# Dividing a kernel's softmax exponentials between ScalarE and VectorE, by a schedule fixed when the program is built

## The chip, the cores and the metric

One core of a Trainium2 chip runs the whole program. The time is device microseconds of one execution. A time quoted below is the median of a kernel's runs; all runs of both kernels, and of every experiment timed in rounds, were in the fast state. Two experiments were run once only, so that their state is unknown. TensorE is called PE, its weight loads PEld, VectorE DVE, ScalarE ACT, GpSimd POOL, and SyncE, which issues most transfers, SP.

## The reference

Four layers on x of 2048 x 512: spectral, attention, spectral, attention, each with a layernorm ahead and a residual add behind. The spectral layers do not change. The attention has 32 query heads of 16 columns and a single key and value head:

```python
def _B_ref(x, wq, wk, wv, wo):
    B, S, D = x.shape            # 1, 2048, 512
    H = 32
    Dh = D // H                  # 16
    q = (x @ wq) ...             # to (B, H, S, Dh)
    k = x @ wk
    v = x @ wv
    scores = jnp.einsum("bhqd,bkd->bhqk", q, k) * (Dh ** -0.5)
    p = _softmax(scores, axis=-1)
    o = jnp.einsum("bhqk,bkd->bhqd", p, v)
    return o ... @ wo
...
x = x + _A_ref(_layernorm(x, axis=-1), A_w_r, A_w_i)
x = x + _B_ref(_layernorm(x, axis=-1), B_wq, B_wk, B_wv, B_wo)
# and both once more
```

A layer has 32 x 2048 x 2048 exponentials: 2048 units of 128 keys x 512 queries. No maximum is subtracted before the exponential.

## The kernel before

Scores are laid out with keys on the partitions. Three units share one PSUM tile and one exponential; its output is the stationary operand of the value matmuls, whose 17th column sums the denominators. `Kv` holds the 16 key columns in one of eight places with zeros in the other rows, so that a full 128-row matmul gives one head. The tile library orders the instructions.

```python
psc = ctx2.enter_context(tc.tile_pool(name="psc", bufs=2, space=bass.MemoryType.PSUM))
...
for gi0 in range(0, len(units), G):                    # G = 3
    grp = units[gi0:gi0 + G]
    sc = psc.tile([P, G, 512], F32, tag="sc")
    for uj, (pidx, kc, hh, qb) in enumerate(grp):
        ...
        nc.tensor.matmul(sc[:, uj, :], lhsT=Kv[:, v, kc * P:(kc + 1) * P],
                         rhs=QT[:, g, qb * 512:(qb + 1) * 512],
                         start=True, stop=True, skip_group_check=True)
    e = expp.tile([P, G * 512], BF, tag="e")
    nc.scalar.activation(out=e[:, 0:ng * 512], in_=sc[:, 0:ng, :]...,
                         func=ACT.Exp, scale=SCALE)
    for uj, unit in enumerate(grp):
        emit_pv(unit, e[:, uj * 512:(uj + 1) * 512], gi0 + uj)   # 4 matmuls, 17 columns each
```

The output projection comes after all of this, as do the residual adds and the layernorm of the next layer, which takes its square root on ACT:

```python
def layernorm_tile(nc, lnpool, tabs, x_ap, xn_ap, on_act=True, use_pool=False):
    ...  # statistics on DVE, into mv
    nc.scalar.activation(out=rstd, in_=mv[:, 1:2], func=ACT.Sqrt, bias=tabs["eps"], scale=1.0)
    nc.vector.reciprocal(rstd, rstd)
    ...  # nb = -mean * rstd, on DVE
    # then xn = x * rstd + nb: on POOL, ACT or DVE
```

The softmax here doesn't subtract the row's maximum and nothing guards it: scores larger than these inputs give would overflow.

## Time and profile before

| | before |
|---|---|
| median of 4 runs | 2298.5 us (2297.8 to 2299.0) |
| span of the profiled run, granted clock | 2296.3 us, 0.979 |
| start to the first exponential | 193 us |
| exponentials, first and second attention layer | 940 and 942 us |
| from the first layer's last exponential to the second's first | 197 us |
| last exponential to the end | 24.6 us |

The windows view gives, for a stretch of the span, the length, each engine's busy time with its number of instructions in brackets, then the granted PE clock, the DMA share and GB/s. These are the two stretches of exponentials, the second cut a microsecond wide:

```profile
core 0: us, PE busy (x) PEld busy (x) DVE busy (x) ACT busy (x) POOL busy (x), PEclk, DMA share, GB/s
193.00:1133.00 940.00, 776.93 (x10282) 357.87 (x10280) 35.69 (x72) 931.90 (x684) 19.42 (x30) 1.00 0.03 4
1330.00:2273.00 943.00, 776.34 (x10286) 357.87 (x10283) 36.53 (x75) 932.33 (x683) 19.43 (x30) 1.00 0.03 4
```

ACT is 99% busy and DVE 4%. This is the whole case for the change: one engine full, another, which can also do arithmetic on every element, idle beside it.

### The profile page before, as it was taken

What the parts mean: (1) busy time and instruction counts of PE and PEld (TensorE: products, weight loads), DVE (VectorE), ACT (ScalarE), POOL (GpSimd) and SP (SyncE); (2) the same over time, 40 slices, a digit from 0 to 9 for tenths busy, and PEclk for the clock granted to TensorE, in tenths of its full rate; (3) what the DMA queues carried; (4) which work ended last, traced back from release to release, by engine and by line L of the source; (5) the groups of instructions that cost most, each with busy time, mean ns of one, the idle gap of its engine ahead of it and who ended that gap; (6) DMA issues with size and microseconds to landing.
All of it is one profiled execution on the core that took longest, in us unless ns stands there. A gap on an engine that the chain in (4) does not pass through costs nothing.

```text
span 2296.3 us, 49219 instructions
## 1 busy us (share of the span) xinstructions
PE 1883.0 (82%) x22176; PEld 864.0 (38%) x22176; DVE 354.5 (15%) x1019; ACT 2059.4 (90%) x1768; POOL 92.1 (4%) x143
## 2 busy tenths in 40 slices
PE   6798888888888888888787988888888888888887
PEld 3234333333333333333342433343333333333333
DVE  6861000000000000000168500000000000000002
ACT  6448999999999999999864489999999999999995
POOL 2011000000000000000000200000000000000000
PEclk9799999999999999999997999999999999999999
DMA  4000000000000000000000000000000000000001
GB/s 133 0 1 20 4 4 4 4 4 4 4 4 4 4 4 4 4 4 4 4 1 0 10 10 4 4 4 4 4 4 4 4 4 4 4 4 4 4 4 40
DMA packets 46818, 19.12 MB, mean 8 GB/s; under 512 B 37376, under 2 KB 43664, under 8 KB 46608
## 3 DMA queue, kind: packets, MB, share of 16 engines
q1 hardware_dynamic: 42464, 11.11, 2.3%
q0 software_dynamic: 4144, 4.87, 1.4%
q8 instruction: 173, 2.83, 0.5%
q14 instruction: 37, 0.30, 0.0%
HBM read 8.63 MB, written 2.10 MB: 5 GB/s over the span
## 4 chain that ended last, share of the span: by engine, by line
ACT 77%; PE 13%; DVE 6%; issue 4%; DMA 1%; ACTq 0%; POOL 0%; DVEq 0%
ACT e L431 76%; PE ps L253 2%; PE ps L145 1%; PE ps L160 1%; PE ps L158 1%; PE sc L427 1%; PE ps L228 1%; PE pv_new L309 1%; DVE stats L84 1%; PE ps L443 1%; DVE m L204 1%; DVE m L210 1%; DVE m L205 0%; DVE Zpk L206 0%; DVE Zsw L212 0%
## 5 line engine op out<-in xcount | busy, mean ns | idle before, releaser
L431 ACT ACTIVATE e<-sc 128x1536 bf16<-128x1536 f32 (+1 forms) x1366 | 1864.2, 1449 | 24.0 <-PE sc L427 11.0
L427 PE MATMUL sc<-QT,Kv 128*128 128x512 bf16 x4096 | 1107.8, 377 | 11.1 <-ACT e L431 10.1
L410 PE MATMUL pv_new<-vaug,e 128*128 128x17 bf16 x16384 | 625.5, 172 | 318.4 <-ACT e L431 316.1
L410 PEld LDWEIGHTS <-e 128*128 128x128 bf16 x16384 | 502.3, 96 | 968.9 <-ACT e L431 954.9
L427 PEld LDWEIGHTS <-Kv 128*128 128x128 bf16 x4096 | 299.1, 96 | 184.3 <-issue 15.2
L387 DVE RECIPROCAL rden<-pv_new 128x32 f32<-128x32 f32 x32 | 11.5, 358 | 1787.9 <-PE pv_new L410 1787.9
L399 POOL DMA_DIRECT2D OQ<-oTp x64 | 41.4, 651 | 1855.4 <-DVE oTp L396 1853.4
L88 ACT ACTIVATE rstd<-mv,eps 128x1 f32<-128x1 f32 x64 | 17.5, 287 | 57.6 <-DVE mv L86 55.6
L116 PE MATMUL ps<-tab_ident,xn_sb 128*128 128x128 bf16 x256 | 26.7, 275 | 32.1 <-ACT xn_sb L97 18.5
L198 ACT CAST Xs<-ps 128x512 bf16<-128x512 f32 x32 | 18.8, 588 | 37.8 <-DVE m L211 37.5
L158 PE MATMUL ps<-Ppk,tab_C 128*128 128x512 bf16 x128 | 48.5, 379 | 0.0
L160 PE MATMUL ps<-Psw,tab_S 128*128 128x512 bf16 x128 | 48.5, 379 | 0.0
L253 PE MATMUL ps<-tab_C,Dpk 128*128 128x512 bf16 x128 | 48.5, 379 | 0.0
L443 PE MATMUL ps<-WO,OQ 128*128 128x512 bf16 x128 | 36.7, 426 | 11.7 <-DVE x_sb L445 5.3
L196 PE MATMUL ps<-Bpk,tab_ident 128*128 128x512 bf16 x64 | 26.5, 493 | 22.5 <-ACT Xs L200 22.5
L84 DVE BATCH_NORM_STATS2 stats<-x_sb 128x6 f32<-128x512 bf16 x64 | 42.1, 675 | 6.4 <-DMA x_sb<-in_A_x_dram 6.3
L97 ACT ACTIVATE xn_sb<-x_sb,nb,rstd 128x512 bf16<-128x512 bf16 x48 | 37.2, 806 | 5.3 <-DVE nb L91 5.3
L172 ACT ACTIVATE tmp<-ps,tab_TWS 128x512 bf16<-128x512 f32 x24 | 16.5, 687 | 23.9 <-PE ps L160 17.1
L253 PEld LDWEIGHTS <-Dpk 128*128 128x128 bf16 x256 | 25.1, 98 | 30.2 <-DVE Dpk L238 0.4
L116 PEld LDWEIGHTS <-xn_sb 128*128 128x128 bf16 x256 | 21.9, 124 | 37.9 <-ACT xn_sb L97 23.7
L228 PE MATMUL ps<-Zpk,tab_ident 128*128 128x512 bf16 x64 | 26.0, 477 | 11.7 <-DVE Dpk L238 4.4
L255 ACT CAST AT<-ps 128x512 bf16<-128x512 f32 x32 | 18.5, 579 | 18.2 <-PE ps L253 18.2
(89 smaller groups left out, 838.7 us busy)
## 6 DMA issues: line engine op xcount, KB each, us to landing
x_sb<-in_A_x_dram SPq DMA_DIRECT2D x1, 2048.0 KB, 10.7
OQ<-oTp SPq DMA_DIRECT2D x64, 32.0 KB, 2.4
OQ<-oTp POOLq DMA_DIRECT2D x64, 32.0 KB, 2.7
wr_sb<-in_A_w_r_dram SPq DMA_DIRECT2D x1, 1024.0 KB, 6.5
win_sb<-in_A_w_i_dram SPq DMA_DIRECT2D x1, 1024.0 KB, 10.0
out_dram<-x_sb SPq DMA_DIRECT2D x8, 128.0 KB, 1.7
out_dram<-x_sb POOLq DMA_DIRECT2D x8, 128.0 KB, 2.1
wq_sb<-in_B_wq_dram POOLq DMA_DIRECT2D x1, 512.0 KB, 9.0
```

The source lines that it names most:

```text
L84: nc.vector.bn_stats(stats, x_ap)
L97: nc.scalar.activation(out=xn_ap, in_=x_ap, func=ACT.Identity, bias=nb, scale=rstd)
L116: nc.tensor.transpose(ps[:, tt, cc, :], xn_sb[:, r_, t_, cc * P:(cc + 1) * P], ident)
L158: nc.tensor.matmul(ps, lhsT=C512[:, r, m * P:(m + 1) * P], rhs=Ppk[:, rt, :], start=(k == 0), stop=False)
L160: nc.tensor.matmul(ps, lhsT=S512[:, r, m * P:(m + 1) * P], rhs=Psw[:, rt, :], start=False, stop=(r == R - 1))
L228: nc.tensor.matmul(ps, lhsT=lt, rhs=src[:, a, :], start=(k2 == 0), stop=(k2 == T - 1))
L253: nc.tensor.matmul(ps, lhsT=lt, rhs=tab[:, m, :], start=(k == 0), stop=(k == 7))
L399: eng.dma_start(out=OQ[32 * kq:32 * kq + 32, q4, :, 32 * pb:32 * pb + 32], in_=oTp[32 * pb:32 * pb + 32, :, :])
L410: nc.tensor.matmul(pv[:, hh, k * 17:k * 17 + 17], lhsT=eu[:, qq * P:(qq + 1) * P], rhs=vaug[:, kc, :], start=first, stop=last, skip_group_ ...
L427: nc.tensor.matmul(sc[:, uj, :], lhsT=Kv[:, v, kc * P:(kc + 1) * P], rhs=QT[:, g, qb * 512:(qb + 1) * 512], start=True, stop=True, skip_gr ...
L431: nc.scalar.activation(out=e[:, 0:ng * 512], in_=sc[:, 0:ng, :].rearrange("p a b -> p (a b)"), func=ACT.Exp, scale=SCALE)
L443: nc.tensor.matmul(ps, lhsT=OQ[:, q4, k, :], rhs=WO4[:, q4, :], start=(q4 == 0), stop=(q4 == nq - 1))
```

## The change

The intent is to give part of the exponentials to DVE. DVE is given no exponential; it computes a line into int16 whose bits, read as bf16, are approximately a power of two. A second copy, shifted by 64 (half an octave) and weighted in the value matmul, halves the bend of that line's error. Four heads of one key block make a "quad"; a small time model in Python hands each of a layer's 512 quads to ACT or DVE, and pins the order of PE, ACT and DVE instructions to what it worked out. Score matmuls shrink to 64 rows (two can run side by side), value matmuls to 32 output rows (four side by side). Denominators are spread by transfers; projection, residual add and layernorm move into the loop. The core of the diff:

```diff
+NTERM = 2
+SH = (0, 64)
+SW = (1.0, 0.70703125)
+EXP_LN = 0.7317
+Y_MUL = float(SCALE * np.log2(np.e) * 128.0)
+Y_ADD = 127.0 * 128.0
...
+class Plan:
+    NA, ND = 2, 4
+    MM, CHANGE, LAT = 0.217, 0.1, 0.2
+    T_EXP, T_READ, T_16, T_DEN, T_ON = 0.94, 0.61, 0.62, 0.5, 0.7
+    D_RECIP, D_ON = 3.0, 5.0
...
+    def scores(u, out):
+        pin(nc.tensor.matmul(out, lhsT=KT[64 * (i // 2):64 * (i // 2) + 64, 2 * (i % 2) + half, kc * P:(kc + 1) * P],
+                             rhs=QT[64 * (i // 2):64 * (i // 2) + 64, g, qb * 512:(qb + 1) * 512], ...))
+    def pv(u, j, e):
+        pin(nc.tensor.matmul(acc[32 * i:32 * i + 32, :], lhsT=V3[:, kc, j, :], rhs=e, ...))
...
+    def finish(qb, s):
+        pin(nc.scalar.copy(out=den, in_=acc))
+        for i in range(4):
+            nc.sync.dma_start(out=dq[32 * i:32 * i + 32, :], in_=den[32 * i + DH:32 * i + DH + 1, :]...)
+        later.append((st["act"] + M.D_RECIP, lambda: recip(qb, s, den, dq, rb)))
...
+    def score_pair():                       # ACT
+        pin(nc.scalar.activation(out=e, in_=sa, func=ACT.Exp, bias=EXP_LN, scale=SCALE))
+        st["act"] = max(st["act"], done) + M.T_EXP
+    def score_single():                     # DVE
+        pin(nc.vector.tensor_scalar(out=t0[:, n, :], in0=sd, scalar1=Y_MUL, scalar2=Y_ADD, op0=ALU.mult, op1=ALU.add))
+        st["dve"] = max(st["dve"], done) + M.T_READ
+        if n == ND - 1:
+            pin(nc.vector.tensor_scalar(out=t2, in0=t0, scalar1=float(SH[1]), scalar2=None, op0=ALU.add))
+            st["dve"] += M.T_16
...
-            for gi0 in range(0, len(units), G):      # and all that is shown of the kernel before
...
-    wka = const.tile([P, NC, P], BF, name="wka")
+    wka = const.tile([P, NC, 4, P], BF, name="wka")   # key projection four times, once per placement
```

`pin` keeps an instruction at its place in the program's order. The numbers in `Plan` are what the time model believes; they change no instruction, only the order and the split.

## The prediction

> **What bounds the kernel now.** I read the page's shares first, then the chain of waits that ends last, then the groups, then the timeline of two microseconds in mid-attention. The page's head and its chain:
>
> ```profile
> PE 1883.0 (82%) x22176; PEld 864.0 (38%) x22176; DVE 354.5 (15%) x1019; ACT 2059.4 (90%) x1768; POOL 92.1 (4%) x143
> ...
> ACT  6448999999999999999864489999999999999995
> ...
> ACT 77%; PE 13%; DVE 6%; issue 4%; DMA 1%; ACTq 0%; POOL 0%; DVEq 0%
> ```
>
> ACT is full in two long plateaus, the two attention layers, and is 77% of the chain. DVE is idle there (a 0 in nearly every slice). The groups, with shapes kept apart, say which instruction it is and what PE does meanwhile:
>
> ```profile
> L431 ACT ACTIVATE e<-sc 128x1536 bf16<-128x1536 f32 x1364 | 1862.3, 1450 | 24.0 <-PE sc L427 11.0 <-PE pv_new L410 9.7 <-ACT e L431 1.9
> L427 PE MATMUL sc<-QT,Kv 128*128 128x512 bf16 x4096 | 1107.8, 377 | 11.1 <-ACT e L431 10.1 <-DVE vaug L341 1.0
> L410 PE MATMUL pv_new<-vaug,e 128*128 128x17 bf16 x16384 | 625.5, 172 | 318.4 <-ACT e L431 316.1
> ...
> L431 ACT ACTIVATE e<-sc 128x1024 bf16<-128x1024 f32 x2 | 2.0, 1017 | 0.0
> ```
>
> The exponentials of 4096 units of 128x512 (2048 a layer) are the bound: in all that time ACT idled 24.0 us, while the value matmuls waited 316 us for it. The timeline of the steady state gives the period:
>
> ```profile
> 599.47 5.54 ACT L431 ACTIVATE e<-sc 128x1536 bf16<-128x1536 f32 x4
> ...
> 601.26 0.34 PEld L427 LDWEIGHTS <-Kv 128*128 128x128 bf16 x3
> 601.29 0.81 PE L427 MATMUL sc<-QT,Kv 128*128 128x512 bf16 x3
> 602.33 0.37 PEld L410 LDWEIGHTS <-e 128*128 128x128 bf16 x12 [0.73 <-ACT e L431]
> 602.34 0.46 PE L410 MATMUL pv_new<-vaug,e 128*128 128x17 bf16 x12 [0.24 <-ACT e L431]
> ```
>
> Score bursts start at 601.29 and 602.65, so three units cost 1.36 us, 0.455 each; an exponential of 1450 ns overlaps its neighbour by about 0.09. The first exponential of layer one starts at 192.99 and the last ends at 1132.83; in layer two they run from 1329.91 to about 2271.7. That is 940 + 942 = 1882 us of attention core, and 2298 - 1882 = 416 us of everything else.
>
> **What the skill says.** Four places bear on it.
> - "VectorE: DVE Perf Modes", section "The perf-mode tier table": a one-source operation on 16-bit data in SBUF runs at four elements a cycle, while fp32 from PSUM gets one. The trace agrees: a 128x4096 bf16 tensor_scalar takes 1227 ns, a 128x512 cast out of PSUM 692 ns.
> - "TensorEngine Tiling (Array Packing)", "Key Properties": tiles run independently, but changing the tiling mode drains the engine. Nothing before shows it, as all its matmuls are 128*128.
> - "TensorE: Matmul & The Clock Gate", "Measured speedup vs the span model": four row tiles gave 3.07 times and three column tiles 2.38 times, not 4 and 3. Not seen here either.
> - "ScalarE: Activation LUTs", "What ACT_TABLE_LOAD costs": 1283 ns for a load plus 1380 ns of drain. The trace has 1283 ns for the load, but no drain beside it: the last exponential ends at 1132.83, the load runs from 1132.85 for 1.28 us; another, from 180.00, is followed by an exponential at 181.30. I use 1.3 us.
>
> **The change part by part.**
>
> (a) Exponentials. Four heads of one key block and query block form a quad; there are 512 quads a layer. A greedy schedule, fixed when the program is built, gives each to ACT or to DVE. On ACT a quad is two activations of 128x1024: 1.017 - 0.09 = 0.93 us each (its source constant says 0.94), so 1.88 us. On DVE it is four linear maps out of PSUM into int16 (the bits are read back as bf16, a piecewise-linear power of two) and one 128x2048 add of 64 that makes a second, half-octave-shifted copy. Rows: 692 ns for 512 columns from PSUM; two back-to-back residual adds took 1.29 us, so consecutive ones cost about 0.61. The 2048-column add by the 4096-column row: (1227 - 160)/2 + 160 - 80 of overlap = about 0.61. A DVE quad is 4 x 0.61 + 0.61 = 3.05 us. ACT alone did a quad in 1.82. Together: 1/1.88 + 1/3.05 = 0.86 quads a microsecond, 595 us a layer if neither ever waits.
>
> (b) Added work on those two engines, a layer: on ACT 32 copies of the accumulator (0.5 each) and 12 query copies (0.5), 22 us; on DVE 32 normalisations (0.69), 32 small reciprocals (0.2) and 12 of the 16 residual adds inside the loop (0.68), 37 us, plus in the first attention layer the layernorm's statistics (675 + 166 + 152 + 198 ns, 12 times, 14 us). DVE's old reciprocal, multiply and transpose work (58 us in all) goes, but was hidden.
>
> (c) TensorE. Scores become 64-row matmuls, two of which can run at once; value matmuls become 32-column ones with 512 moving columns, four at once, a term for ACT units and two for DVE units. 512 columns at full clock take 0.217 (3.69 us for 16 in the old key projection is 0.23 with its edges). ACT quad: 2 x 0.217 + 0.217 = 0.65. DVE quad: its scores are issued one per free slot, often unpaired, 4 x 0.217, + 2 x 0.217 = 1.30. At the ratio of (a), 0.62 DVE quads to an ACT quad, that is 1.46 us per 1.88 us. With perhaps three mode changes in that time at 0.1 us (the source's constant) and rows of four at 3.07 rather than 4 times, TensorE asks for 1.46 + 0.3 + 0.15 = 1.9 us. This is an estimate, and it says that TensorE has no slack left: it becomes a third, equally loaded engine that the two others must queue for.
>
> (d) What that does to the slots. DVE has two one-bank score slots. A freed slot needs 0.217 for the matmul and about 0.2 until DVE sees it, against 0.61 until the other slot is used up: 0.19 us of slack, less than a value burst with two mode changes (0.4 or more). ACT has 0.93 - 0.42 = 0.5. So I take DVE at 83% busy and ACT at 93%, both within the time T of a layer. Less the added work (ACT 22, about 3%; DVE 37, about 5%, and 3% waiting on reciprocal transfers, see e): ACT 0.90/1.88 = 0.479, DVE 0.75/3.05 = 0.246; 0.725 quads a microsecond: 706 us a layer.
>
> (e) Transfers. The denominators go through four one-row transfers, a reciprocal, a store to DRAM and a broadcast read. SP takes 1.26 us to issue two transfers, and one lands after 2.4 us: the fourth lands at 3 x 0.63 + 2.4 = 4.3 us, where the schedule puts the reciprocal at 3.0. The store and read, 2 x 2.4, about fill their allowed 5.0. About 1 us of DVE waiting in 32 stages is the 3% above.
>
> (f) Table loads. Projection and layernorm now run inside the loop. In the first attention layer each of 12 square roots falls among exponentials: 2 x 1.3 + 0.29, and 0.8 for the normalising activation: 12 x 3.7 = 44 us on ACT, with the other two engines soon starved behind it. The second layer only writes out.
>
> (g) Edges. Key projection grows from 16 to 64 matmuls: +48 x 0.216 = +10 us a layer; the query projection up front stays at 16; the key rearrangement by transfers (3.1 us) goes. At the end 1132.8 to 1160.5, 28 us, becomes the last denominator chain (0.6 + 4.3 + 0.2 + 5 + 0.7) and four projections of 8 matmuls (8 us), 19 to 20 us: -8. Edges come to about 0.
>
> Sum: 416 + 706 + (706 + 44) = 1872; I say 1870 us, 19% less.
>
> **Rivals.**
> - Packed matmuls do not overlap, and TensorE becomes the bound: per layer 2048 x 0.217 + 2048 x 1.36 x 0.217 = 444 + 604 = 1050 us, plus changes, so about 1150: 416 + 2300 = 2700 us. For: nothing before shows overlap. Against: the skill's measured packing. I give it 3%.
> - The schedule works nearly as planned, both elementwise engines 95% full: 595/0.95 + 25 = 650 a layer, 44 less hidden: 1740 us. For: the source's constants agree with my rows. Against: (c) leaves TensorE no room, and order is fixed on all engines, so one late operand holds everyone.
> - Waits replace the bound: each schedule slip (reciprocal at 3.0 instead of 4.3, layernorm among exponentials) stalls three in-order engines at once, each some 75% busy: 780 a layer, 2020 with table loads of 60.
> - Hidden anyway? No: the exponential is on the path itself, and the spectral layers, which don't change, are only 416.
>
> **Range and chances.** Between the second and third rival lie 1740 and 2020; I hold 1740 to 2000 for 8 in 10. A gain under 2% would need 910 us a layer, ACT and DVE each at about 65%: 2%. Slower needs the first rival: 3%. Faster by over 2%: 95%.
>
> **What would show it.** In the changed profile: about 1290 activations of 128x1024 at 1017 ns (a figure near 1110 would mean that the bias costs a pointer read); DVE at 0.69 busy for 512 columns and near 0.69 for the 2048-column add, which shows the four-a-cycle mode; score matmuls of the two halves starting within some nanoseconds; over 20 table loads, nearly all in the first attention layer, which should be some 45 us longer than the second. DVE should wait mostly for score matmuls, and the reciprocal for its four transfers. I am wrong if ACT falls below 80% in the second attention layer (a stall I have not seen), if a mode change costs much over 0.1 us, or if the first layer is no longer than the second.

## The result, and the profile after

| | before | after |
|---|---|---|
| median (number of runs) | 2299.0 us (12) | 1850.6 us (8) |
| lowest and highest | 2297.0 to 2301.4 | 1845.3 to 1856.7 |
| ratio | | 0.805 (95%: 0.8037 to 0.8062) |

A ratio is the mean time of one kernel's runs over that of the other's of the same rounds, so it is not quite the ratio of the medians. The prediction said 1870 us; the time is 19.5% lower. The page of the changed kernel, the lines that answer to those the prediction shows of before (the last is the chain that ended last, followed back from the last instruction, at each step to what released it; "issue" is time in which an engine waited for nothing that the profile shows, and SPq is SP issuing transfers):

```profile
PE 1603.7 (87%) x11584; PEld 512.2 (28%) x11584; DVE 1501.6 (81%) x2846; ACT 1516.7 (82%) x1842; POOL 33.8 (2%) x48
...
DVE  5785599978897789879966955999898989788995
ACT  5544699989998999989965435999899989898995
...
PE 34%; ACT 26%; DVE 16%; DMA 14%; issue 7%; SPq 2%; DVEq 0%; ACTq 0%
```

DVE is now as full as ACT in the two plateaus, and the chain that ended last, once 77% ACT, passes from engine to engine: no single engine sets the end. The groups, shapes kept apart (busy time in us, mean ns of one, idle time of the engine just before them and what ended it):

```profile
L488 ACT ACTIVATE e<-sa 128x1024 bf16<-128x1024 f32 x1312 | 1243.9, 1039 | 63.6 <-PE sa L400 52.5 <-PE sd L400 6.8
L505 DVE TENSOR_SCALAR t<-sd 128x512 int16<-128x512 f32 x1472 | 937.7, 682 | 75.0 <-PE sd L400 50.8 <-PE sa L400 10.6
L511 DVE TENSOR_SCALAR t<-t 128x2048 int16<-128x2048 int16 x368 | 255.5, 694 | 12.7
L400 PE MATMUL sa<-QT,KT 64*128 64x512 bf16 x2624 | 598.8, 385 | 69.5 <-ACT e L488 56.3 <-DVE V L349 1.0
L400 PE MATMUL sd<-QT,KT 64*128 64x512 bf16 x1472 | 535.9, 381 | 51.3 <-DVE t L505 47.1
L413 PE MATMUL acc_new<-t,V 128*32 128x512 bf16 x2944 | 247.4, 384 | 0.4 <-DVE t L511 0.4
```

ACT did 1312 activations for 328 quads a layer, DVE 1472 reads and 368 adds for 184 quads a layer. DVE waits mostly for its own score matmuls (`sd`), and the score matmuls for ACT (`sa`) or DVE (`sd`) to free a slot: the engines queue for each other. The timeline of a few microseconds shows the packing; its columns are start, length, engine, line, what, and the count of instructions merged:

```profile
220.80 0.39 PE L400 MATMUL sa<-QT,KT 64*128 64x512 bf16 x2
220.95 2.65 DVE L505 TENSOR_SCALAR t<-sd 128x512 int16<-128x512 f32 x4
...
222.28 0.37 PE L400 MATMUL sd<-QT,KT 64*128 64x512 bf16 x1
...
223.63 0.69 DVE L511 TENSOR_SCALAR t<-t 128x2048 int16<-128x2048 int16 x1
...
224.21 0.40 PE L413 MATMUL acc_new<-e,V 128*32 128x512 bf16 x4
224.43 0.60 PE L413 MATMUL acc_new<-t,V 128*32 128x512 bf16 x8
...
224.97 0.39 PE L400 MATMUL sa<-QT,KT 64*128 64x512 bf16 x2
```

Two score matmuls of 64 rows take 0.39 us, one alone 0.37: they run side by side. A round of four value matmuls starts 0.22 us before the next: four run in the time of one. Three rounds from 224.21 would end the streaming at 224.21 + 3 x 0.217 = 224.86, and the next score matmul starts at 224.97, so a change of mode costs about 0.1. Four DVE reads take 2.65 us, 0.66 each, where both the plan and the prediction had 0.61. The mean hides where that comes from. By the starts of single instructions in the trace (medians over all 368 quads) the four reads follow at 0.60, 0.73 and 0.61 us: the third waits for its score, as the first two used up both slots. The add starts 0.72 after the last read, whose result it needs.

Where the time went, by the first and last exponential of each layer (the profiled runs, in us; the prediction gave the edges as one sum):

| stretch | before | predicted | after |
|---|---|---|---|
| start to first exponential | 193.0 | | 214.2 |
| first attention loop | 940 | 750 | 727.5 |
| between the layers | 197.1 | | 200.9 |
| second attention loop | 942 | 706 | 680.7 |
| end | 24.6 | | 22.6 |
| the three edges together | 415 | 416 | 437.7 |

Both loops are some 24 us shorter than predicted and the edges 22 us longer: the total was right to 1% partly because these cancel. The windows of the two loops, of a clean stretch of the second, and of a stretch of the second with projections:

```profile
214.20:941.80 727.60, 637.18 (x4974) 181.68 (x4970) 628.06 (x1042) 683.84 (x747) 0.00 (x0) 0.97 0.04 13
1142.60:1823.40 680.80, 628.47 (x4970) 181.53 (x4970) 613.59 (x994) 638.59 (x699) 3.33 (x6) 0.99 0.05 16
1150.00:1230.00 80.00, 75.83 (x617) 21.38 (x611) 77.47 (x127) 79.36 (x89) 0.00 (x0) 1.00 0.04 12
1310.00:1350.00 40.00, 35.68 (x260) 11.03 (x258) 31.53 (x52) 30.52 (x34) 1.18 (x2) 0.96 0.09 28
```

In the clean stretch ACT is 99% busy, DVE 97% and PE 95%. Where the projections of a finished query block come between, all of them fall to 76 to 89% together. The average of the second loop is ACT 94%, DVE 90%.

### The profile page after: what moved, and what is told of

Same layout as the page of the kernel before. It is cut to its first block, busy times and chain, and to the rows that moved or that the text cites. A ratio compares the mean times of both kernels' runs of the same rounds, so it can differ in the third digit from the quotient of the medians.

```text
span 1845.9 us, 30297 instructions
## 1 busy us (share of the span) xinstructions
PE 1603.7 (87%) x11584; PEld 512.2 (28%) x11584; DVE 1501.6 (81%) x2846; ACT 1516.7 (82%) x1842; POOL 33.8 (2%) x48
## 4 chain that ended last, share of the span: by engine, by line
PE 34%; ACT 26%; DVE 16%; DMA 14%; issue 7%; SPq 2%; DVEq 0%; ACTq 0%
ACT e L488 23%; DMA rb<-rd 7%; DVE t L505 7%; PE acc_new L413 6%; PE sa L400 6%; PE sd L400 5%; PE ps L259 3%; DMA rd<-dq 3%; PE ps L473 3%; DMA dq<-den 2%; SPq L429 2%; PE ps L334 2%; PE ps L151 2%; PE ps L166 1%; PE ps L164 1%
## 5 line engine op out<-in xcount | busy, mean ns | idle before, releaser
L488 ACT ACTIVATE e<-sa 128x1024 bf16<-128x1024 f32 x1312 | 1243.9, 1039 | 63.6 <-PE sa L400 52.5
L505 DVE TENSOR_SCALAR t<-sd 128x512 int16<-128x512 f32 x1472 | 937.7, 682 | 75.0 <-PE sd L400 50.8
L400 PE MATMUL sa<-QT,KT 64*128 64x512 bf16 x2624 | 598.8, 385 | 69.5 <-ACT e L488 56.3
L400 PE MATMUL sd<-QT,KT 64*128 64x512 bf16 x1472 | 535.9, 381 | 51.3 <-DVE t L505 47.1
L400 PEld LDWEIGHTS <-KT 64*128 64x128 bf16 x4096 | 208.5, 94 | 624.6 <-issue 593.1
L413 PE MATMUL acc_new<-e,V 128*32 128x512 bf16 x2624 | 307.4, 392 | 2.1 <-ACT e L488 1.7
L511 DVE TENSOR_SCALAR t<-t 128x2048 int16<-128x2048 int16 x368 | 255.5, 694 | 12.7
L413 PE MATMUL acc_new<-t,V 128*32 128x512 bf16 x2944 | 247.4, 384 | 0.4 <-DVE t L511 0.4
L413 PEld LDWEIGHTS <-V 128*32 128x32 bf16 x5568 | 128.2, 94 | 359.7 <-issue 323.6
L473 PE MATMUL ps<-WOp,on_next 128*128 128x512 bf16 x192 | 50.9, 417 | 27.1 <-DVE on_next L460 18.3
```

What stands on the lines that cost most here:

```text
L400: pin(nc.tensor.matmul(out, lhsT=KT[64 * (i // 2):64 * (i // 2) + 64, 2 * (i % 2) + half, kc * P:(kc + 1) * P], rhs=QT[64 * (i // 2):64 * ...
L413: pin(nc.tensor.matmul(acc[32 * i:32 * i + 32, :], lhsT=V3[:, kc, j, :], rhs=e, start=first, stop=False, skip_group_check=True))
L473: pin(nc.tensor.matmul(ps, lhsT=on[:, s, qt * P:(qt + 1) * P], rhs=WOp[:, s, :], start=(s == 0), stop=(s == 7)))
L488: pin(nc.scalar.activation(out=e, in_=sa, func=ACT.Exp, bias=EXP_LN, scale=SCALE))
L505: pin(nc.vector.tensor_scalar(out=t0[:, n, :], in0=sd, scalar1=Y_MUL, scalar2=Y_ADD, op0=ALU.mult, op1=ALU.add))
L511: pin(nc.vector.tensor_scalar(out=t2, in0=t0, scalar1=float(SH[1]), scalar2=None, op0=ALU.add))
```

## The experiments

The twelve runs were made in three batches, each on one chip beside the kernel before. "The loop" is first to last exponential of a layer. The changed kernel itself is 1850.6 us with loops of 727.5 and 680.7. The same program, profiled again in the third batch (experiment 10), had loops of 735.1 and 683.3 and its first exponential at 211.5 instead of 214.2. So a single profile can't tell differences of some 8 us in the first loop, or of 3 in the others, from chance.

### 1. Are the table loads what makes the first loop longer? (e1_newton)

In the first attention layer 12 of the 16 layernorms fall among exponentials. Their square root is replaced by a bit-trick seed on DVE and two Newton steps on POOL; the normalising activation stays on ACT.

```diff
-    nc.scalar.activation(out=rstd, in_=mv[:, 1:2], func=ACT.Sqrt, bias=tabs["eps"], scale=1.0)
-    nc.vector.reciprocal(rstd, rstd)
+    nc.vector.tensor_scalar(out=y.bitcast(I32), in0=v.bitcast(I32), scalar1=-0.5, scalar2=1597463007.0, ...)
+    for it in range(2):     # y = y * (1.5 - 0.5 * v * y * y), four operations on nc.gpsimd
```

> The changed kernel, with the square root of the 12 layernorms inside the first attention loop replaced: the seed by two small DVE operations, two Newton steps and the bias on POOL, so that ACT keeps only exponentials, copies and the normalising activations in the loop. Theory (step f): the table loads and the ACT waits round them lengthen the first attention layer by 44 us; table loads fall from 28 to 4, the first layer (727.5 us from first to last exponential) falls to the second's 681 plus at most 10 for the normalising activations, 685 to 695, and the time to about 1812. Rival: the loads fall into gaps in which ACT would wait for scores anyway, because the projections hold TensorE; then the layer loses less than 15 us and the time stays above 1835.

Measured: correct, 1851.2 us (1850.2 to 1858.0), ratio to before 0.8053 [0.8030, 0.8076]; loops 729 and 684. The table loads fell from 28 to 4, and nothing was gained. The timeline of ACT at the first of these layernorms, in the changed kernel:

```profile
396.87 1.28 ACT L94 ACT_TABLE_LOAD   x1
399.69 0.29 ACT L94 ACTIVATE rstd<-mv,eps 128x1 f32<-128x1 f32 x1 [1.54 <-DVE mv L92]
400.47 0.81 ACT L103 ACTIVATE xn_sb<-x_sb,nb,rstd 128x512 bf16<-128x512 bf16 x1 [0.48 <-DVE nb L97]
401.30 1.28 ACT L488 ACT_TABLE_LOAD   x1
```

and of this run at the same place, DVE's statistics, POOL's last step and ACT:

```profile
396.04 0.18 DVE L92 BATCH_NORM_AGGREGATE mv<-stats 128x2 f32<-128x6 f32 x1
398.91 0.26 POOL L107 TENSOR_SCALAR nb<-mv,rstd 128x1 f32<-128x1 f32 x1
399.20 0.81 ACT L117 ACTIVATE xn_sb<-x_sb,nb,rstd 128x512 bf16<-128x512 bf16 x1 [5.60 <-POOL nb L107]
```

The bracket is the engine's idle time before the instruction and what ended it. ACT still stood there, now 5.60 us for the normalisation's operand instead of loading tables. (Over the run this wait came 12 times, 51.8 us in all.) ACT's queue is in order, and the plan put the layernorm behind a projection whose add and statistics were not yet done. Here the first table load lay in the shadow of that wait. But the edit did not only remove the loads: the statistics are there at 396.22, and the root's nine small operations on POOL take until 399.17, longer than the root on ACT had taken. Summed over the twelve layernorms of the loop, ACT's stops, from the exponential before to the next one, went from 64.1 us to 60.4, though 30.8 us of loads had gone. So the run shows that ACT stands there about as long either way; what the loads alone would be worth it does not show.

### 2. Take the layernorm out of ACT's queue (e6_pool_norm)

The previous edit, and the normalisation of those 12 tiles on POOL as well, so that nothing in ACT's loop waits for DVE's statistics:

```diff
-   use_pool=(nxt == "B" and k % 2 == 0)
+   use_pool=((nxt == "B" and k % 2 == 0) or (layers[li] == "B" and len(seen) <= 12))
```

> The run with the Newton steps, and the normalising activation of the same 12 tiles moved from ACT to POOL, so that no layernorm instruction stands in ACT's queue in the loop. Theory now: it is not the table loads that lengthen the first attention layer but ACT's queue: the first layernorm instruction in it, whichever it is, waits for the chain projection, residual add, statistics, and the exponentials behind it wait too (51.8 us for 12 in the Newton run). Then the first layer falls from 727 to 680 to 695 us and the time to about 1810. Rival: the layer is longer because of DVE's added 14 us of statistics and TensorE's clock (0.97 against 0.99): then it stays above 710 and the time above 1835.

Measured: correct, 1820.5 us (1818.1 to 1824.8), ratio 0.7914 [0.7901, 0.7927]; loops 696.3 and 687.4. The first loop lost 31 us and is within 9 us of the second, as this theory says. So most of the first loop's extra comes from the layernorm's place in ACT's in-order queue, with what it does there and what it waits for. This run took both away together, so that how much of the 31 us belongs to the loads and how much to the waits is not shown.

### 3. All exponentials to ACT (e2_all_act)

The schedule, packing and transfers stay, but no quad goes to DVE:

```diff
-        if not dve_units and quads and allowed(quads[-1]) and d_slots[0] <= st["t"] + 0.3:
-            take(dve_units, NTERM)
```

> The changed kernel with every quad given to ACT; DVE gets none, everything else stays. Theory: the split of the exponentials is the gain. 512 quads x 1.88 us = 963 us a layer, plus 25 of copies on ACT and 44 of table loads in the first: about 2450 us in all, slower than the kernel before by 6%, as an activation of 1024 columns is dearer per unit (0.47) than one of 1536 (0.455). Rival: the packed matmuls, not the split, took away waits; then the time would stay well under 2299.

Measured, one run of unknown state: correct, 2522.6 us; loops 1063 and 1021 us. The rest of the change without the split is 224 us slower than the kernel before: activations of two units cost more per unit than those of three (ACT is busy 0.472 us for a unit, 0.455 before), and the edges are longer. The whole gain is the split. A window of its first loop:

```profile
700.00:740.00 40.00, 35.46 (x168) 7.21 (x167) 1.20 (x3) 39.84 (x44) 0.00 (x0) 0.50 0.03 8
```

ACT is full. PE seems 89% busy, but at a granted clock of 0.50: it was given half speed and still kept up. This matters for reading such a page: PE's busy share here says nothing about its need.

### 4. How much room has TensorE? (e3_full_rows)

Scores of 128 rows, which cannot pair. The result is wrong (four heads' rows are added up; relative error 0.75); the instruction count and the plan are unchanged.

```diff
-        lhsT=KT[64 * (i // 2):64 * (i // 2) + 64, 2 * (i % 2) + half, kc * P:(kc + 1) * P],
-        rhs=QT[64 * (i // 2):64 * (i // 2) + 64, g, qb * 512:(qb + 1) * 512],
+        lhsT=KT[:, 2 * (i % 2) + half, kc * P:(kc + 1) * P],
+        rhs=QT[:, g, qb * 512:(qb + 1) * 512],
```

> The changed kernel with score matmuls over all 128 rows instead of 64, in the same order, so that two can't run side by side (wrong result on purpose: each sums two heads). Theory (step c): TensorE has no slack left; each of the 656 pairs a layer takes 0.217 us more, 142 us a layer, and most of it shows: 1850 + 200 to 300 = 2050 to 2150 us. Rival: TensorE waits for free score slots often enough to hide it; then under 1900.

Measured, one run of unknown state: 1965.9 us; loops 788 and 741, each 60 us longer. An ACT pair now takes two slots of 0.217 instead of one: 656 pairs a layer, 142 us of added PE work, of which 60, or 42%, showed. A clean stretch:

```profile
1210.00:1250.00 40.00, 39.53 (x274) 13.19 (x277) 35.38 (x57) 36.54 (x40) 0.00 (x0) 1.00 0.03 8
```

Now PE is the engine at 99%, and ACT and DVE are at 91 and 88%. So pairing carries the schedule, but in the changed kernel PE had slack for more than half of this extra work; the prediction's "TensorE has no slack left" was too strong. The result lies between the two expectations.

### 5. The planned waits for the transfers (e5_margins)

```diff
-    D_RECIP, D_ON = 3.0, 5.0
+    D_RECIP, D_ON = 5.0, 7.0
```

> The changed kernel with the schedule's allowances for the denominator transfers raised from 3 to 5 us (reciprocal) and from 5 to 7 us (normalisation), so that DVE meets them later in its order. Theory (step e, as sized): 1 us of DVE waiting in each of 64 stages, some 30 us of it on the path: about 1820 us. Rival, from the waits of the changed kernel: in the two loops DVE waited 13.3 us for the first transfers and 16.5 us for the broadcast, and the other two engines have work queued meanwhile: 10 us at most, 1840 or more.

Measured: correct, 1844.5 us (1842.5 to 1845.7), ratio 0.8021 [0.8009, 0.8033]; loops 727.2 and 670.6. Alone it gave 6 us, and none of it in the first loop. It did take the waits away: DVE's for these transfers, in the two loops, fell from 31 us to 1.6, and the transfers and their issue from 16% of the chain that ended last to 4%. So a share of that chain is no measure of what its removal gains: when one wait went, others ended last in its place. Experiment 11 returns to that.

### 6. The edges (e8_edges)

The key projection runs twice instead of four times for a block, and a per-partition mask makes the four placements while the result is copied out; four PSUM buffers there; the attention weights' loads are issued on SP behind the spectral weights.

```diff
-                for half in range(4):
+                for pair in range(2):
...
+                    for v in (2 * pair, 2 * pair + 1):     # ACT for pair 0, DVE for pair 1
+                        nc.scalar.activation(out=dst, in_=ps, func=ACT.Copy, scale=tabs["KMASK"][:, v:v + 1])
...
-        nc.gpsimd.dma_start(out=wka[:, :, 2 * (i // 2 % 2) + i % 2, 16 * i:16 * i + 16], in_=wk_v)
+        nc.sync.dma_start(out=wka[:, :, 16 * i:16 * i + 16], in_=wk_v)
```

> The changed kernel with cheaper edges: the key projection made twice per query block instead of four times and masked per partition while it is copied out (32 matmuls a layer instead of 64, four PSUM slots instead of two), and the weight loads for attention put behind the spectral weights on the same queue. Theory: the stretch from the table load at 186.5 to the first exponential at 214.2 falls from 27.7 us by about 12 in each layer (a query block takes 5.88 us there now, of which 3.7 are key matmuls), and the start by 4 us (the second spectral weight lands at 33.4 us and holds DVE's queue): 1850 - 28 = about 1822. Rival: the copies, now with a scale, become the bound there and the start is set by the table loads: less than 10 us, above 1840.

Measured: correct, 1835.5 us (1832.9 to 1838.2), ratio 0.7983 [0.7971, 0.7995]. The first exponential came at 197.2 instead of 214.2 and the stretch between the layers fell by 8.5 us, but the loops grew by 9 and 5 us. The edges' extra 22 us were thus real and could be taken back. Whether the loops really gave half of it up again is not shown: against the changed kernel's second profile (735.1 and 683.3) they are only 2 us longer each, and runs of one kernel differ by up to 11 us among each other (the changed kernel's by 1845 to 1857).

### 7. One term instead of two (e4_one_term)

No second copy and no second value matmul: DVE's quad loses its add and PE a quarter of its value matmuls (4096 are left of 5568). It is less exact.

```diff
-NTERM = 2
+NTERM = 1
-EXP_LN = 0.7317
+EXP_LN = 0.0385
...
-            pin(nc.vector.tensor_scalar(out=t2, in0=t0, scalar1=float(SH[1]), scalar2=None, op0=ALU.add))
-            st["dve"] += M.T_16
```

> The changed kernel with one term of the DVE exponential instead of two: no add of 64, one value matmul for a DVE unit, and the ACT bias set to the mean of the one term (0.0385), so the result is less exact. Theory (steps a and c): a DVE quad falls from 3.05 to 2.44 us and TensorE's share from 1.30 to 1.08; 1/1.88 + 1/2.44 = 0.94 quads a microsecond, 543 us a layer if nothing waits; at the 0.87 of the ideal that the second layer of the changed kernel reached (595 of 681) that is 622: about 60 us less a layer, 1730 us. Rival: TensorE alone bounds the loop; its saving is only 0.22 us on each of 184 DVE quads plus the mode changes, about 45 us a layer at most and less as DVE takes more quads with unpaired scores: above 1780.

Measured: correct, 1835.5 us (1826.7 to 1840.1), ratio 0.7971 [0.7945, 0.7998]; loops 739 and 661. A window of the second loop shows both elementwise engines below their earlier shares of 94 and 90%, at 93 and 81%:

```profile
1150.40:1811.80 661.40, 596.60 (x4220) 161.15 (x4233) 537.10 (x870) 611.94 (x669) 3.35 (x6) 0.98 0.05 17
```

DVE is busy 77 us less in this loop (614 to 537), and the loop is 20 us shorter; the first is 11 us longer (4 against the changed kernel's second profile). The amount of DVE's work is not what bounds the loops. What grew is DVE's wait for the transfers, in the two loops from 31 us to 68, and their share of the chain that ended last:

```profile
PE 36%; DMA 24%; ACT 17%; DVE 12%; issue 6%; SPq 5%; DVEq 0%; ACTq 0%
```

Experiment 12 shows what the same edit brings where, among other things, these waits are gone.

### 8. The add dropped (e7_no_add)

The same question with less changed: the second value matmul stays and re-reads the first copy (wrong, relative error 0.066); the plan's clock drops the add too.

```diff
-            pin(nc.vector.tensor_scalar(out=t2, in0=t0, scalar1=float(SH[1]), scalar2=None, op0=ALU.add))
-            st["dve"] += M.T_16
-            for j, tt in ((0, t0), (1, t2)):
+            for j, tt in ((0, t0), (1, t0)):
```

> The changed kernel without the add of 64: the second value matmul reads the first copy again, so TensorE's work per DVE quad stays and DVE's falls from 3.05 to 2.44 us (less exact on purpose). Theory (step d): DVE is held by the turn-round of its two score slots (0.42 us of matmul and latency against 0.61 us of reading), and the add is just the time in which they refill; without it DVE idles instead: 1835 us or more, DVE's busy share in the second layer falling from 90% to about 80%. Rival: DVE's own work is the bound; then 0.61 us less on 184 quads, about 112 us of DVE work a layer, shows as 40 us a layer or more: under 1780.

Measured: 1919.2 us (1909.7 to 1924.4), ratio 0.8342 [0.8316, 0.8368]: 69 us slower, with less work. Loops 761 and 724. The waits (engine, line, what it waited for; us in total, times, longest) have all grown:

```profile
ACT e L488 <- PE sa L400: 140.8, 223, 4.2
PE sd L400 <- DVE t L505: 136.7, 186, 3.5
DVE t L505 <- PE sd L400: 113.7, 168, 4.3
```

The theory that DVE's slots bound it had expected no gain, but no loss of this size either. Since the plan's clock had lost the add as well, the order and the split had changed along with the work: 201 DVE quads a layer instead of 184. The two had to be taken apart. The transfers are another candidate: DVE waited for them 112 us in the loops, against 31 in the changed kernel, and the chain that ended last is

```profile
PE 41%; DMA 26%; DVE 14%; ACT 10%; SPq 5%; issue 4%; DVEq 0%; ACTq 0%
```

### 9. The add dropped, the order kept (e9_same_order)

As before, except that the plan still counts 0.62 us for the add. Counted in the traces, this run has the same number of PE instructions and of bursts of score and value matmuls (774 and 760) as the changed kernel; experiment 8 had 798 and 788.

```diff
-            pin(nc.vector.tensor_scalar(out=t2, in0=t0, scalar1=float(SH[1]), scalar2=None, op0=ALU.add))
             st["dve"] += M.T_16
-            for j, tt in ((0, t0), (1, t2)):
+            for j, tt in ((0, t0), (1, t0)):
```

> Wrong on purpose, like the earlier run without the add: the add of 64 is dropped and the second value matmul re-reads the first copy. But here the planner's own clock still counts the 0.62 us of the add, so that the order of the TensorE's instructions and the split of the quads (328 to ACT, 184 to DVE a layer) stay exactly those of the changed kernel; only the 368 adds of 0.69 us are gone. Theory (the earlier loss of 69 us came from the plan that the missing add made, which gave DVE 17 more quads a layer that its PSUM slots cannot turn round in time): the time returns to that of the changed kernel or somewhat under it, 1810 to 1855 us, with DVE near 75 percent busy in the loops. Rival (the loss came from the chip: a second matmul on the same copy, or DVE finishing in another rhythm than ACT): it stays slow, over 1890 us.

Measured: wrong (relative error 0.040), 1848.7 us (1841.4 to 1851.6), ratio 0.8031 [0.8013, 0.8049]; in the same rounds the changed kernel had 1858.7 us and 0.8082. Two windows, the loops:

```profile
210.10:941.90 731.80, 627.86 (x4972) 185.49 (x4969) 513.71 (x858) 682.92 (x747) 0.00 (x0) 0.96 0.04 13
1144.60:1825.20 680.60, 613.32 (x4972) 183.90 (x4969) 499.39 (x810) 637.39 (x699) 3.34 (x6) 0.99 0.05 16
```

DVE's busy time fell by 114 us in each loop (628 to 514, 614 to 499), and the loops are nearly as long as the changed kernel's (731.8 and 680.6, against 735.1 and 683.3 in the same batch). In time it is 10 us faster than the changed kernel in the same rounds, and the two intervals do not meet, so of the 228 us of DVE's work about 10 showed. With this order, then, the add lies almost wholly in slack, and a saved microsecond of DVE turns into a wait (its reads' idle time rose from 75.0 to 259.9 us). Experiment 8's loss is the plan's, not the chip's: nearly the same instructions, in the split and the order that the plan makes for a cheaper DVE, cost 70 us. What in that plan costs so much is not settled. 52 more changes of mode in the whole run at 0.1 us would be 5 us. Waits for the transfers are a rival that was not tested: here DVE waits 84 us for them in the loops without harm, with 114 us of each loop free, while experiment 8, whose plan had given that time to more quads, waits 112. It would take experiment 8 with the longer margins of experiment 5, and no such run was made.

### 10. The changed kernel again (e12_after_again)

> The changed kernel itself, unaltered, on the same chip as these runs: 1845 to 1857 us as before, with 12 table loads in the first attention loop; it gives the ratio of the combined kernel to it from the same rounds of the kernel before.

Measured: 1858.7 us (1854.6 to 1859.7), ratio 0.8082 [0.8070, 0.8094], just over the expected range (and 24 table loads in the first loop, as in the first profile, where the expectation says 12). Its first batch had 0.805. So the same program differs by 0.4% between batches, on different chips, and the two intervals do not meet: the 6 us of experiment 5 are at the edge of what such a comparison carries.

### 11. The three helpful parts together (e10_combined)

The layernorm on POOL, the longer margins and the cheaper edges (experiments 2, 5 and 6) in one kernel.

> The three parts that helped alone, together: no layernorm work in ACT's queue inside the attention loops (alone -30 us), key projection twice instead of four times a block with the attention weights' loads behind the spectral ones (alone -15), and the longer waits planned for the reciprocal and the normalisation (alone -6). If they act in different places, as the theory says (queue order inside the loop; the edges; DVE's queue): about 1800 us, range 1785 to 1815. Rival (the loops take back what an edge gives, as the edges run showed by 13 of its 26 us): 1815 or more.

Measured: correct, 1775.8 us (1771.2 to 1777.8), ratio 0.7722 [0.7709, 0.7735]; against the changed kernel of the same rounds 0.7722 / 0.8082 = 0.955. Alone the parts gave 30, 15 and 6 us; together 75 against the first batch's median and 83 against the same rounds. Its two loops:

```profile
195.60:874.70 679.10, 625.56 (x4965) 185.15 (x4962) 625.00 (x1044) 635.66 (x697) 34.89 (x120) 1.00 0.05 14
1070.00:1741.50 671.50, 625.01 (x4965) 185.43 (x4962) 612.37 (x996) 635.91 (x697) 3.46 (x6) 1.00 0.05 16
```

The first loop is now within 8 us of the second. Against experiment 2, which differs by the margins inside the loop and by the edges outside of it, the loops are shorter by 17 and 16 us. The margins alone (experiment 5) gave 0 in the first loop and 10 in the second. The likely reading is that in the first loop the layernorm's stalls ended last as long as they were there. DVE did wait for transfers in that loop, 18 us against 13 in the second, and in experiment 5 these waits went without any gain. No run had the margins and the layernorm's move without the edges, so this stays a reading. The granted clock of the loops is another difference that no run separates: 1.00 in both here, 0.99 in experiment 2, and 0.97 and 0.99 in the changed kernel.

### 12. One term on top of it (e11_combined_one_term)

> The combined kernel with one term of the exponential instead of two (less exact, it passed before): alone the one term gave -15 us. If DVE's 0.69 us add and the second value matmul were partly hidden behind ACT's queue stalls and now set the pace, the gain is larger than 15 here: 1760 to 1785 us. Rival (the DVE slots bound it, as before): 1785 to 1800.

Measured: correct, 1681.3 us (1679.4 to 1682.5), ratio 0.7313 [0.7302, 0.7324]. The same edit that gave 15 us alone gives 95 here, more than either expectation. Windows of its two loops:

```profile
196.00:834.40 638.40, 590.94 (x4236) 164.62 (x4233) 545.30 (x914) 608.44 (x671) 31.28 (x120) 1.00 0.05 15
1027.50:1656.60 629.10, 590.63 (x4236) 164.96 (x4233) 532.34 (x866) 608.13 (x671) 3.45 (x6) 0.99 0.06 17
```

The exponentials run for 638 and 629 us, against 739 and 661 in experiment 7. ACT is at 95 and 97% and DVE at 85%. Between 215 and 830 us, ACT's waits for the layernorm's statistics went from 30.5 us (experiment 7) to none and DVE's for the projections from 41.8 to 16.9. DVE's waits for the transfers, in both loops, went from 68 us to 0.2, and DMA from 24% of the chain that ended last to 1%. Three things changed between the two runs, so how much of the 95 us is the margins' is not shown. The two-term version of experiment 11 keeps the changed kernel's exponential.

## Why the prediction was right or wrong

The predicted time, its direction and its range held. That the time is within about 1% is in part luck: the loops' and the edges' errors cancel. The mechanism held in the main: the split of the exponentials is the gain (experiment 3), two and four matmuls do run side by side, no engine sets the end alone, and waits for score matmuls head DVE's list. Step by step:

- **(a), the exponentials: the idea right, DVE's quad too short.** ACT's pairs follow each other at about 0.95 us (a quad 1.9, predicted 1.88). DVE's four reads take 2.65 us and a quad 3.29, from one add at 220.34 to the next at 223.63, where the prediction said 3.05. Its rows were right (reads in a row follow at 0.60); what it left out is the third read's wait for a score slot, 0.13, and that the add needs the last read, 0.1. The ideal would be 1/1.9 + 1/3.29 = 0.83 quads a microsecond, 617 us a layer, not 595.
- **(b), added work: right.** A loop has 25 us of copies on ACT (predicted 22) and 37 us of normalisations, reciprocals and residual adds on DVE (predicted 37).
- **(c), TensorE: too strict.** Rounds of four value matmuls follow at 0.22 us, a full factor of four where the step had 3.07. The change of mode at 0.1 was right. The sentence "TensorE has no slack left" failed: 58% of 142 us of added PE work a layer vanished into slack (experiment 4, a single run).
- **(d), the slots: wrong in form, about right in sum.** The step had DVE at 83% and ACT at 93% evenly; the second loop has 90 and 94%. But clean stretches run at 97 and 99%, and the losses sit where projections come between. And DVE's busy time, from which the step worked, does not set the loop's length: 114 us of it a loop can go almost without moving it (experiment 9). The order is fixed, and within it ACT is busy 639 of the second loop's 681 us; only 42 us are left for ACT to wait. The turn-round of DVE's two slots does cost DVE something, by the third reads' 0.13 us some 24 us a loop (184 x 0.13, an estimate). Whether it holds ACT is not excluded: dropping the add leaves the reads, and so the slots, as they were. The step's form, a busy share for each engine on its own, is what failed.
- **(e), the transfers: too large.** The step had about 64 us of DVE waiting in both loops. In the loops DVE waited 13.3 us for the four transfers and 18.1 for the broadcast (both loops summed; experiment 5's expectation has 16.5, without the last query block), and longer margins alone saved 6 us, perhaps some 30 beside the layernorm's removal (experiment 11).
- **(f), table loads: the size about right, the account incomplete.** The first loop is 47 us longer (52 in the second profile), predicted 44, with 24 loads in it. ACT's instructions for the twelve layernorms add up to just the 44 us of the step. But ACT stops for 64 us there, the other 20 being waits for the layernorm's operands, which the step did not have. Exchanging the loads for a longer chain on POOL changed the stops little (64 to 60 us) and the time not at all (experiment 1); taking the layernorm out of ACT's queue gave 31 us (experiment 2). The term was summed as costs on ACT alone; the runs show a stop of an in-order queue made of costs and waits.
- **(g), the edges: too small by 22 us.** The start alone grew by 21 us (18 in the second profile). The step counted the 48 more key matmuls at 0.216, 10 us, and let the end and the dropped transfers make up for it; by its own items (twice +10, -3 or twice that, -8) it should have said +6 to +9, not 0, and the end, -8 there, gave 2. A block of the new key projection takes 5.88 us (198.40 to 204.28), 3.7 of it key matmuls; transposes, four groups of matmuls and copies out of PSUM share two buffers there. The second spectral weight, loaded beside the attention weights, came at 33.4 us, and DVE waited 5.0 us for it. Experiment 6, which changed all of this at once, took 25 us off these stretches.

Of the rivals, "packed matmuls do not overlap" fell at the first look at the timeline. "Nearly as planned" describes the clean stretches and, with the combined kernel's loops of 679 and 671, what repair of the queues comes near to. "Waits replace the bound" described the first loop rightly in kind: the layernorm's stop held ACT and then the others, but its removal was worth 31 us and the loop was 727.5, not 780 or more. (With "table loads of 60" that rival's own sum is 416 + 2 x 780 + 60 = 2036, not 2020.)

Of the signs to look for, ACT at 94% in the second loop, 28 table loads, DVE at 0.68 and 0.69, the change of mode and the longer first loop came as said. Two did not quite: the activations took 1039 ns, not 1017, but far from the 1110 that it named; and there are 1312 of them, where the prediction said 1290 and the split of its step (d) would give 1353.

## What to carry to other kernels

An idle engine that can do the bottleneck's arithmetic, even crudely, can take a fifth off the time, as here. But once several in-order engines run near 95% in a fixed order, a saved microsecond on one may become a wait (experiment 9), and a new plan may even lose (experiment 8). Then look not for the costliest instruction but for the instruction in a busy queue that waits for a slow chain (here a layernorm among exponentials), and move it to a queue that has time: exchanging its cost for a longer chain, in the same place of the queue, gained nothing. Test parts together as well as alone, for one stall can hide another's worth: 30 + 15 + 6 became some 80, and 15 became 95.

## What the Trainium skill lacked or had wrong

- "TensorE: Matmul & The Clock Gate", "Measured speedup vs the span model": three column tiles at 2.38 times. It gives none for four. Here four column tiles of 32 with 512 columns, issued in rounds, start a round every 0.22 us, the time that one such matmul adds (0.217): four times, sustained over rounds. A share of the tiles lost to packing, as the prediction took from there, was not seen.
- "TensorEngine Tiling (Array Packing)", "Key Properties": says that changing the mode drains the engine, without a cost. Here it was 0.09 to 0.10 us: the median time from the last start before a change to the first after it, less the 0.217 of a matmul, over 742 changes each way.
- "ScalarE: Activation LUTs", "What ACT_TABLE_LOAD costs": 1380 ns of drain beside the 1283 ns of the load. At 401.30 the load took 1.28 us and the exponential behind it started at 402.60, 0.02 us after: no drain is seen here. What a load costs the kernel is another matter: 24 loads fewer, with a longer chain in their place, changed the time by nothing that can be measured (ratio 0.8053 for 0.8049).
- No page that I read has what the runs turn on: that with an order fixed at build time over three in-order engines, 114 us less work a loop on one of them can come back almost whole as waits (experiment 9), and that another split and order of nearly the same program can cost 70 us (experiments 8 and 9).
